# Another order of a hand-written list of stages, with some 70 stages on another engine, in an attention and two-MoE-block kernel on one core

## The chip, the cores and the metric

The kernel runs on one core of one Trainium2 chip. The metric is the device time of one execution in microseconds; 674.87 us is the median of three runs of the kernel before (674.87, 674.87 and 677.03).

The names of the engines in the rows: PE is TensorE (matrix products), PEld its weight loads, DVE is VectorE, ACT is ScalarE, POOL is GpSimd, and SP is SyncE, whose queue issues all transfers here.

## The reference, cut to what matters

Attention with four batches, eight heads, 512 local and 32 global rows of head size 64, and then two feed-forward blocks one after the other on all 2304 rows of width 512. A local row sees the local rows up to 32 places away and the 32 global ones; a global row sees all rows of its batch.

```python
s_g = scale * np.matmul(q_g, k_all.transpose(0, 1, 3, 2))
out_g = np.matmul(sm(s_g), v_all)
s_ll = np.where(np.abs(pos[:, None] - pos[None, :]) <= 32, s_ll, -1e9)
out_l = np.matmul(sm(np.concatenate([s_lg, s_ll], -1)), np.concatenate([v_g, v_l], axis=2))
...
h = x @ w_in                       # 512 -> 1024
solu = h * sm(h)
ln = (solu - mu) / np.sqrt(var + 1e-06) * g_ln
x = ln @ w_out                     # 1024 -> 512
...
h = x @ w2_in                      # 512 -> 2048
g = np.where(h >= 1, h, np.where(h <= -1, 0.0, (h + 1) ** 2 / 4))
out = g @ w2_out                   # 2048 -> 512
```

## The kernel before, in words

The 2304 rows are 17 tiles of 128: sixteen of local rows (four to a batch) and one with all global rows. A step is the work of one tile. For a tile's step the kernel does the attention, the first product of the first block (h, into two banks of PSUM), a softmax and a layer norm of it, transposes of the result, and, for two tiles at a time, the second product (y). The second feed-forward block follows after all tiles, from about 300 us on; it is not touched.

The float products run as three products of a high and a low part. A weight comes as a pair of words and has to be converted on the chip, piece by piece: 16 pieces of 128 x 1024 words, eight of the first weight (0 to 3 for the first half of h, 4 to 7 for the second) and eight of the second weight (8 to 15; 16 to 18 belong to the next block). The function `conv` (L166) has the steps of a piece: A strips the sign, C clamps, B shifts, D sets the sign and the exponent's top, F brings in bits of the lower word, m multiplies by the norm's gain (second weight only), H rounds to the high part, L subtracts it, which leaves the low part.

The tile framework orders most queues by itself, but up to the eighth step a list written out by hand, `SCRIPT` (L52), sets the order on every queue at once. It is read from the left, and `issue` (L945) issues each name's instructions, so each engine's queue has its own stages in the order of the list; across engines only data and buffers wait. (The list goes on into the ninth to fourteenth tile, since tiles ahead are prepared.) A name is a kind and a tile's number (a piece's number for A to L). A last letter v puts the stage on VectorE where it has a choice; without it the stage is on GpSimd (C, L, xl), or on ScalarE (A, H, Gc, Pa, Pb, xh, tha, thb). For Rn, Ie, ze, bn and nn it is the other way round: v puts them on ScalarE, without it they are on VectorE. The kinds that matter here:

- loads, on SyncE: q (scores' inputs of a tile, 0.85 MB), qg, v (values of a tile's windows, 1.05 MB, two buffers), vn (values of a batch), w (a piece, 0.52 MB), s and o for the next block's pieces. Three pieces in eight go to buffers of the pool, the others into rooms of the tensor xy, which later tiles and pieces use again (`ROOMS`, L80).
- attention: S scores (64 small products), M mask, R row maximum, Rn its scaling, Ea and Eb the exponentials of half the heads each, Ie and I the inverse of the sums, Ta and Tb transposes, Pa and Pb their copies, V the product with the values, X the norm, XT a transpose by blocks into xy. The same for the global rows: G scores, Gc their copy, gm, gn, ge, gi, gt, gp, gc, gv, go.
- first block: xh and xl the two parts of a tile of x; ha and hb the halves of h with the high part of x (eight products each), hA and hB with the low part (four each); mx maximum, ex exponential, ze and z inverse of the sum, u the product with h, bn, pw and nn the layer norm; ta and tb transposes, tha, thb, tla, tlb their high and low parts; ya, Ya, yb, Yb the quarters of y for two tiles, yca and ycb their copies.
- Z: three products of zeros on TensorE (`keep_warm`, L272).

Scores and h share two banks pairs of PSUM (the pool psH, `scores` L342, `hmm` L521): S and ha take them in turn, and wait until the last reader of the tile before the last is done, Eb for scores and u for h. G, T, V, gt, gv and the transposes take three other banks in turn (psA). The lines of the rows: L149 is every ScalarE activation but A, L140 most of VectorE's stages, L173 to L190 the steps of `conv`, L351 S, L404 and L406 G, L417 T, L432 V, L529 h, L270 y, L492 gv.

Of the kernel before, what the change touches and what calls it, by code (L numbers as in the profile page):

```python
# [1281 lines left out]
```

## Time and profile before

| what | us |
| --- | --- |
| median of three runs | 674.87 |
| lowest and highest | 674.87 and 677.03 |
| span of the profiled execution, first to last instruction | 673.8 |

| engine | busy us | share of the span | instructions |
| --- | --- | --- | --- |
| VectorE | 432.9 | 64% | 766 |
| ScalarE | 369.5 | 55% | 918 |
| GpSimd | 259.8 | 39% | 293 |
| TensorE weight loads | 577.5 | 86% | 6092 |

Matrix products are pipelined and their ends in the trace are modelled, so TensorE's busy time counts small gaps as work; its starts can be trusted, and its weight loads show how full it is. The list covers TensorE's first 160 us. In the page's 40 slices TensorE is busy 7, 6, 8 and 9 tenths in the first four and 9 or more from there on; VectorE is at 7 to 9 tenths in the first six slices, and the transfers move 321 to 358 GB/s in the first five.

### The profile page before, as it was taken

What the parts mean: (1) busy time and instruction counts of PE and PEld (TensorE: products, weight loads), DVE (VectorE), ACT (ScalarE), POOL (GpSimd) and SP (SyncE); (2) the same over time, 40 slices, a digit from 0 to 9 for tenths busy, and PEclk for the clock granted to TensorE, in tenths of its full rate; (3) what the DMA queues carried; (4) which work ended last, traced back from release to release, by engine and by line L of the source; (5) the groups of instructions that cost most, each with busy time, mean ns of one, the idle gap of its engine ahead of it and who ended that gap; (6) DMA issues with size and microseconds to landing.
All of it is one profiled execution on the core that took longest, in us unless ns stands there. A gap on an engine that the chain in (4) does not pass through costs nothing.

```text
span 673.8 us, 15103 instructions
## 1 busy us (share of the span) xinstructions
PE 655.2 (97%) x6089; PEld 577.5 (86%) x6092; DVE 432.9 (64%) x766; ACT 369.5 (55%) x918; POOL 259.8 (39%) x293
## 2 busy tenths in 40 slices
PE   7689999999999999999999999999999999999997
PEld 3467888989899889999999998998888888988986
DVE  5989987776787679654887679455655453333332
ACT  4888987556554244345666554554444466344443
POOL 2343463121112114203444676356776655222321
PEclk8979999999999999999999999999999999999999
DMA  8988854425752613301665341663333465744522
GB/s 321 358 348 333 343 203 159 165 65 164 288 193 92 254 32 125 95 1 32 187 188 186 128 125 63 217 220 126 125 126 125 134 210 190 237 136 157 170 81 80
DMA packets 29686, 114.24 MB, mean 170 GB/s; under 512 B 3376, under 2 KB 3888, under 8 KB 27056
## 3 DMA queue, kind: packets, MB, share of 16 engines
q1 hardware_dynamic: 29616, 113.28, 48.4%
q8 instruction: 48, 0.79, 0.5%
q14 instruction: 22, 0.18, 0.1%
HBM read 88.88 MB, written 24.38 MB: 168 GB/s over the span
## 4 chain that ended last, share of the span: by engine, by line
PE 90%; DMA 5%; DVE 3%; issue 1%; ACT 1%; SPq 0%; ACTq 0%
PE acc L270 26%; PE h L270 25%; PE yT L270 14%; PE h L529 13%; DMA vw<-in_vwin_dram 2%; PE plnT L594 2%; PE o L432 2%; DMA qkT<-in_qk_dram 2%; PE S L351 2%; PE pPT L417 2%; PE y L270 1%; PE og L492 1%; DVE xy L140 1%; PE G L404 0%; DVE w L180 0%
## 5 line engine op out<-in xcount | busy, mean ns | idle before, releaser
L270 PE MATMUL acc<-wo,g 128*128 128x512 f32 x816 | 211.3, 393 | 0.0
L270 PEld LDWEIGHTS acc<-wo,g 128*128 128x128 f32 x816 | 149.8, 188 | 23.2
L164 POOL TENSOR_TENSOR g<-xy,g 128x384 fp32r<-128x384 f32 (+1 forms) x65 | 62.8, 974 | 139.8 <-ACT g L149 122.4
L149 ACT ACTIVATE xy<-xy 128x384 f32<-128x384 f32 (+1 forms) x144 | 72.7, 505 | 71.5 <-DVE xy L140 68.5
L529 PE MATMUL h<-win,x 128*128 128x512 f32 x408 | 101.3, 400 | 0.0
L270 PE MATMUL yT<-lnT,wout 128*128 128x256 f32 x768 | 95.7, 284 | 0.0
L270 PEld LDWEIGHTS yT<-lnT,wout 128*128 128x128 f32 x768 | 93.4, 189 | 0.9
L529 PEld LDWEIGHTS h<-win,x 128*128 128x128 f32 x408 | 74.8, 188 | 15.9
L140 DVE TENSOR_TENSOR xy<-h,xy 128x384 f32<-128x384 f32 (+1 forms) x64 | 33.5, 524 | 62.1 <-PE h L270 60.9
L777 POOL TENSOR_TENSOR g<-xy,g 128x192 fp32r<-128x192 f32 x60 | 51.4, 876 | 54.2 <-ACT g L149 46.9
L149 ACT ACTIVATE g<-xy 128x384 fp32r<-128x384 f32 (+1 forms) x96 | 48.0, 500 | 18.7 <-DVE xy L140 16.7
L270 PE MATMUL h<-yT,w2i 128*128 128x384 f32 (+1 forms) x300 | 56.4, 334 | 0.0
L149 ACT ACTIVATE xy<-h 128x384 f32<-128x384 f32 (+1 forms) x64 | 30.0, 469 | 46.2 <-PE h L270 46.2
L270 PE MATMUL h<-yT,S 128*128 128x384 f32 (+1 forms) x288 | 54.9, 325 | 0.0
L270 PEld LDWEIGHTS h<-yT,w2i 128*128 128x128 f32 x300 | 52.5, 188 | 2.3
L140 DVE SCALAR_TENSOR_TENSOR xy<-h,xy 128x384 f32<-128x384 f32 (+1 forms) x48 | 26.1, 545 | 43.9 <-ACT xy L149 43.7
L270 PEld LDWEIGHTS h<-yT,S 128*128 128x128 f32 x288 | 48.8, 188 | 5.5 <-DVE xy L140 1.7
L149 ACT ACTIVATE e<-S,nm 128x128 f32<-128x128 f32 x128 | 45.3, 379 | 8.0 <-PE plnT L594 4.3
L571 POOL TENSOR_TENSOR rstd<-rstd,nhalf 128x1 f32<-128x1 f32 x17 | 11.4, 668 | 82.8 <-DVE rstd L140 49.6
L517 POOL TENSOR_TENSOR x<-xy,x 128x512 fp32r<-128x512 f32 x15 | 19.8, 1323 | 43.6 <-ACT x L149 35.5
L270 PE MATMUL h<-yT,lnT 128*128 128x384 f32 (+1 forms) x180 | 34.0, 334 | 0.1
L140 DVE SCALAR_TENSOR_TENSOR xy<-xy 128x384 f32<-128x384 f32 (+1 forms) x48 | 28.9, 602 | 7.8 <-ACT xy L149 7.8
(147 smaller groups left out, 1059.3 us busy)
## 6 DMA issues: line engine op xcount, KB each, us to landing
vw<-in_vwin_dram SPq DMA_DIRECT2D x16, 1024.0 KB, 7.0
wo<-w2d_o SPq DMA_DIRECT2D x32, 512.0 KB, 3.7
qkT<-in_qk_dram SPq DMA_DIRECT2D x15, 832.0 KB, 7.4
wraw<-in_w2i_dram SPq DMA_DIRECT2D x16, 512.0 KB, 3.7
wraw<-in_w2o_dram SPq DMA_DIRECT2D x16, 512.0 KB, 4.2
w2d_o<-wo SPq DMA_DIRECT2D x16, 512.0 KB, 5.1
w2d_s<-S SPq DMA_DIRECT2D x16, 512.0 KB, 5.5
S<-w2d_s SPq DMA_DIRECT2D x16, 512.0 KB, 5.9
```

The source lines that it names most:

```text
L140: self.last = getattr(nc.vector, name)(*args, **kw)
L149: vec.act = nc.scalar.activation(**kw)
L164: eng.tensor_tensor(out=lo, in0=src, in1=hi.bitcast(F32), op=ALU.subtract)
L270: mm(out=dst, lhsT=pairs[i][0][x], rhs=pairs[i][1][y], start=start and j == 0, stop=stop and j == 3 * n - 1, **kw)
L351: mm(out=S[32 * hp:32 * hp + 32, par, ci], lhsT=qT[r, hp, ci], rhs=kT[r, hp, w:w + 4].rearrange("p c d -> p (c d)"), start=True, stop=True)
L417: nc.tensor.transpose(ps[:, hp], eT[t][:, HP * par + hp], ident)
L432: mm(out=o[rows, ci, par], lhsT=PT[t][:, par, ci, rows], rhs=w[:, ci, D * h:D * h + D], start=True, stop=True)
L517: eng.tensor_tensor(out=xT[t][1], in0=x[:, :, n:n + P], in1=xT[t][0].bitcast(F32), op=ALU.subtract)
L529: mm(out=hps[t][:, half], lhsT=x[i][:, k], rhs=win[j][:, k, sl], start=not lo and j == 0 and k == 0, stop=lo and k == KD - 1)
L571: nc.gpsimd.tensor_tensor(sts[t].rstd, sts[t].rstd, nhalf, ALU.pow)
L594: nc.tensor.transpose(ps[:, k], ln[t][:, P * c:P * c + P], ident)
L777: eng.tensor_tensor(out=out, in0=x, in1=y, op=ALU.subtract)
```

## The change

The list holds the same 629 names, each once (and Z eight times), in another order on all queues, and 69 of them have their last letter added or taken away, so that these stages run on another engine of the two that they can use. The loads begin with pieces 0 and 5 and then the first tile's q; before, q of the first tile came first. Nothing else is changed: the same sums from the same values. The functions called are the same.

```diff
@@ -50,31 +50,32 @@
 SCRIPTED = 8
 
 SCRIPT = """
-Z0 q0 Z0 w0 qg0 S0 q1 w2 Z0 G0 w5 Gc0 S1 M0 A0v C0 R0 Rn0 B0 D0 F0 A2v Z0 G1 q2 M1 R1 C2 B2 D2 Ea0
-A5 v0 Rn1 Z0 C5 B5 H0 Ta0 Eb0 F2 Ea1 Z0 Pa0 S2 Gc1 G2 Gc2 M2 Eb1 D5 H2 F5 R2 q3 L0v L2v Z0 Z0 G3
-Gc3v Tb0 Ie0v w4 Rn2v I0 H5v Pb0 A4 C4 L5 V0 Ta1 Ea2 w1 S3 gm0 Pa1 A1v X0 Tb1 w7 Ie1v gn0 ge0 XT0 B4
-q4 qg1 Eb2 xh0 C1 A7v gt0 B1 M3 C7 q5 xl0 D4 B7 Pb1 gp0 D1 R3 F1 D7 F4 v1 G4 n0 S4 w6 H4v M4 w3 Rn3v
-Ie2v Ea3 Gc4 Ta2 Eb3 L4 V1 F7 H1 R4 I1 A6 Tb2 L1 H7 Pa2 S5 C6 Rn4v X1 v2 G5 Pb2 A3v L7 I2 XT1 q6 M5
-B6 Ea4 Ta3 C3 B3 Gc5 Eb4 R5 V2 v3 Tb3 S6 Rn5v D3 Ie4v X2 Pa3 Pb3 F3 w9 D6 H3v w11 G6 Gc6v Ea5 M6
-Ie3v Tb4 Eb5 F6 V3 I3 R6 w14 L3 XT2 A9v q7 H6 Ta4 X3 Pa4 L6 ha0 Rn6v v4 xh1 v5 A14 Ea6 C9 gi0 XT3 B9
-hb0 Pb4 D9 hA0 Eb6 hB0 C14v B14 F9 G7 Ta5 Gc7 Tb5 V4 mx0 v6 D14 w8 ex0 F14 m9 Ie6v S7 ze0 I6 z0 I4
-Pa5 u0 Pb5 M7 bn0v Ta6 xh2 pw0 X4 V5 Ie5v R7 Rn7v ha1 Ea7 gm1 Pa6 gn1 A11v XT4 Eb7 xl1 H9 Tb6 q8 I5
-m14 C11 hb1 hA1 vn0 gc0 L9 w10 nn0v hB1 xl2v B11 ha2 xh3 D11 mx1 ta0 F11 X5 hb2 ex1 ge1 A8v hA2 hB2
-H14v L14 ze1 tha0 z1 u1 tla0 Pb6 tb0 qg2 C8v m11 mx2 Ie7v V6 XT5 A10v bn1v thb0 gv0 pw1 S8 ex2 tlb0
-X6 v7 go0 ze2v z2 u2 nn1v Ta7 w13 gt1 B8 Pa7 C10 I7 xh4 xl3 D8 ta1 gp1 B10 H11 F8 ha3 m8 L11 tha1 M8
-v8 tb1 bn2v q9 Tb7 R8 thb1 H8 hb3 L8 hA3 Rn8v qg3 A13 D10 tlb1 w12 tla1 w15 Ea8 pw2 hB3 gc1 F10 XT6
-mx3 s0 ya0 nn2 m10 Pb7 G8 Eb8 ex3 C13 B13 V7 Gc8 D13 X7 H10 ze3v G9 F13 z3 Gc9 S9 A12v Ie8v Ta8 L10
-A15 u3 M9 bn3v R9 m13 xl4 C15 q10 Ya0 C12 tb2 B12 q11 ha4 s1 vn1 yca0 ta2 Pa8 hb4 Rn9 H13 thb2 hA4
-D12 F12 Ea9 B15 m12 tha2 D15 hB4 tla2 tlb2 Tb8 F15 G10 L13 Eb9 A16 H12v Gc10v mx4 S10 I8 L12 M10 s2
-Pb8 m15 G11 A17 XT7 v9 V8 pw3 Gc11 X8 v10 yb0 ex4 H15 ze4v C17 Ta9 L15v z4 Yb0 R10 Ie9v u4 xh5 nn3v
-bn4v C16v I9 ycb0 Pa9v ta3 XT8 xl5 pw4 gm2 ha5 Rn10 tha3 tb3 hb5 nn4 B17 gi1 hA5 hB5 tla3 B16 Ea10
-Eb10 thb3 Tb9 S11 xh6 Pb9 mx5 ex5 V9 ze5v tlb3 ta4 xh7 tha4v z5 u5 Ie10v A18 ya1 tb4 ha6 Ya1 v11 M11
-bn5v hb6 X9 xl6v D16 D17 R11 F16 F17 hA6 gn2 yca1 Rn11 C18v H16v Ea11 tla4 Ta10 hB6 yb1 Eb11 thb4
-tlb4 xh8v Tb10 q12 mx6 Pa10 B18 pw5 xl8 XT9 ge2 Pb10 I10 Ie11 D18 gv1 ex6 nn5v V10 ze6v X10 S12 Ta11
-q13 z6 Yb1 M12 F18 go1 Pa11 u6 tb5 R12 ycb1 thb5v ha7 tlb5 gt2 L16 hb7 ta5 gp2 tha5 bn6 gc2 Tb11 I11
-Rn12 xl7 pw6 H18v tla5 hB7 hA7 ya2 Ea12 nn6 Eb12 G12 Pb11v mx7 Gc12v S13 G13 ex7 gi2 Gc13v M13 Ie12v
-v12 V11 q14 o0 tb6 thb6 L18 ze7 Ya2 ta6 z7 R13 Rn13v Ea13 Eb13 s3 xd0 u7 xd1 tlb6 XT10 H17v tha6
-bn7v tla6 L17v Ie13 o1 X11 I12 I13 vn2 yca2 pw7 nn7 v13
+Z0 Z0 w0 w5 q0 A0 C0v B0 D0 qg0 A5 C5 B5 D5 F5 H5v S0 L5 F0 H0 L0 w2 q1 A2 Z0 G0 Gc0 G1 M0 R0 S1
+Rn0v Ea0 Eb0 C2v B2 D2 F2 H2v L2 w1 M1 R1 Ta0 Pa0 Rn1v Gc1v Ea1 q2 Eb1 A1v C1 B1 G2 Gc2 Ie1v q3
+S2 D1 M2 R2 F1 H1v G3 Gc3 w7 L1 A7v C7 gm0 gn0 S3 M3 R3 Rn3 Rn2v Ea2 Tb0 Pb0 Z0 ge0 gi0 Eb2 v0
+V0 w3 A3v C3 Ie0 w4 I0 X0 I1 Tb1 Ta1 XT0 Pa1 Pb1 B7 D7 F7 gt0 H7v Ea3 Eb3 B3 gp0 D3 F3 qg1 q4
+H3v L3 gc0 S4 M4 G4 Gc4 q5 S5 A4 L7 R4 Z0 M5 C4 v1 R5 G5 V1 X1 XT1 xh0 xl0 Gc5 n0 Tb2 Rn4 w14
+A14 C14 Ta2 Pa2v Ie3v B14 D14 F14 v2 Pb2 V2 Z0 Ie2v I2 X2 Ta3 Pa3v q6 m14 G6 Gc6v w6 Ea4 Eb4
+Rn5v Ea5 B4 D4 Ie4 A6v C6 Z0 XT2 Tb3 Pb3 Eb5 Tb4 F4 H4 L4 Ta4 B6 xh1 D6 F6 H6 Z0 S6 M6 R6 v3 V3
+I3 X3 Ie5v L6 ha0 hb0 XT3 Pa4 Pb4 w8 A8v C8 q7 xl1 G7 Gc7v gm1 v4 Rn6v H14 L14 Ea6 Eb6 Ie6v hA0
+hB0 mx0 ex0 V4 Ta5 vn0 S7 I4 X4 XT4 Tb5 Pa5 Pb5 ze0 z0 u0 bn0v gv0 go0 w9 gn1 ge1 A9v w10 M7 R7
+Tb6 Rn7 xh2v w11 A11v C9 pw0 ha1 hA1 hb1 hB1 C11v B11 D11 Ea7 Eb7 F11 w15 B8 D8 v5 V5 F8 nn0v
+qg2 Ta6 mx1 I5 ex1 Pa6 X5 XT5 Pb6 ze1 z1 u1 xh3 ha2 hb2 gi1 B9 m8 ta0 xl2 D9 F9 bn1v pw1 nn1v m9
+I6 v6 v8 tha0v tla0 V6 Ta7 X6 Pa7v q8 hB2 hA2 mx2 vn1 H9v H8 L8 tb0 L9 thb0 tlb0 tb1 thb1 ha3
+tlb1 ta1 tha1v m11 ex2 ze2v z2 tla1 A10 u2 gt1 gp1 Ie7v C10 B10 D10 F10 hb3 G8 xl3 Gc8v H11 v7
+xh4 m10 w12 A12 xl4 bn2v pw2 S8 gc1 hB3 hA3 M8 R8 q9 Rn8v H10v XT6 Tb7 mx3 G9 Gc9v Pb7 Ea8 nn2
+ya0 L10 L11v Ya0 ex3 ze3v z3 tb2 C12 u3 I7 ta2 xh5v Eb8 Ie8 xl5 bn3v pw3 S9 M9 R9 Rn9 tha2v tla2
+ha4 hA4 thb2 tlb2 yca0 w13 A13 Ea9 Eb9 q10 C13 B13 D13 s0 B12 hb4 D12 hB4 F12 m12 G10 Gc10v V7
+X7 xh6 A15 XT7 q11 ha5 Ta8 Pa8 Tb8 Pb8 F13 m13 mx4 ex4 ze4v H12v hA5 Ie9 nn3v I9 hb5 hB5 V8 H13
+C15 B15 D15 I8 X8 G11 L13v L12 yb0 F15 m15 Gc11 Ta9 H15 L15 Pa9 ta3 z4 u4 S10 bn4v Yb0 tha3 M10
+A16 pw4 R10 tla3 Rn10 tb3 thb3v XT8 ycb0 C16v gv1 Tb9 tlb3 mx5 go1 Ea10 Eb10 xh7v ya1 Ya1 v9
+Pb9v V9 s1 A17 gm2 gn2 s2 ex5 xl6 A18 C18 ze5 nn4 tb4 ta4 z5 u5 q12 B18 bn5v D18 F18 X9 XT9 S11
+C17 thb4 yca1 tlb4 qg3 B17 ha6 hb6 hB6 v10 pw5 Ta10 nn5v tha4v tla4 M11 R11 Rn11 Ea11 B16 v11
+hA6 mx6 Tb10 Pa10 Pb10 ex6 D17 F17 H17 Ie10 ge2 D16 Eb11 xd1 F16 ze6 z6 u6 bn6 pw6 yb1 Yb1 I10
+V10 X10 ycb1 Ta11 Pa11v ta5 tha5v tla5 q13 S12 gt2 ha7 M12 R12 tb5 gp2 gc2 gi2 hb7 XT10 thb5v
+tlb5 L17 G12 nn6 Gc12v xl7 H18 hA7 Rn12v Ea12 L18v Eb12 Ie12 Ie11v xh8 xl8 hB7 mx7 S13 M13 Tb11
+G13 xd0 Gc13v H16 ya2 L16 ex7 ze7v z7 u7 Pb11 bn7v pw7 o0 R13 tb6 ta6 q14 tha6v nn7 v12 Rn13v
+I11 o1 I12 tla6 V11 X11 thb6v tlb6 Ya2 s3 Ea13 Eb13 Ie13 I13 v13 vn2 yca2
 """
 
 ROOMS = [2, 3, 4, 0, 1, None, None, None, 2, 3, 4, 0, 1, None, None, None]
```

## Rows read from the trace of the kernel before

**Rows 1.** The page's busy time of each engine: us, share of the span, instructions.
```profile
PE 655.2 (97%) x6089; PEld 577.5 (86%) x6092; DVE 432.9 (64%) x766; ACT 369.5 (55%) x918; POOL 259.8 (39%) x293
```

**Rows 2.** Stretches: us, busy us by engine (PE, PEld, DVE, ACT, POOL), clock, DMA share, GB/s.
```profile
60.00:160.00 100.00, 99.88 (x1585) 87.98 (x1585) 82.48 (x156) 69.12 (x210) 36.65 (x35) 1.00 0.54 198
...
14.00:35.00 21.00, 14.36 (x415) 9.46 (x415) 19.76 (x37) 19.11 (x85) 6.58 (x8) 0.99 0.94 362
35.00:42.00 7.00, 5.93 (x142) 4.71 (x145) 5.08 (x10) 5.13 (x23) 3.32 (x4) 0.51 1.00 409
42.00:60.00 18.00, 16.24 (x437) 12.72 (x426) 17.77 (x37) 15.57 (x58) 5.14 (x6) 1.00 0.75 295
```

**Rows 3.** TensorE's timeline: start us, us, line, what, count, idle before and its releaser.
```profile
36.07 0.58 PE L432 MATMUL o<-vw,PT 128*32 128x64 f32 x10 [2.31 <-issue]
...
46.66 5.86 PE L529 MATMUL h<-win,x 128*128 128x512 f32 x24
...
54.96 1.10 PE L432 MATMUL o<-vw,PT 128*32 128x64 f32 x64 [0.83 <-DMA vw<-in_vwin_dram]
...
59.71 2.14 PE L529 MATMUL h<-win,x 128*128 128x512 f32 x8
...
135.08 0.65 PE L492 MATMUL og<-vn,PgT 128*32 128x64 f32 x32
...
136.74 1.10 PE L432 MATMUL o<-vw,PT 128*32 128x64 f32 x64
```

**Rows 4.** VectorE's timeline, the same columns (M0, F7, X1, M5, D6 to Gc6, F6, u0, gm1, D11).
```profile
6.31 0.70 DVE L140 TENSOR_TENSOR S<-S,masks 128x512 f32<-128x512 f32 x1 [5.20 <-PE S L351]
...
33.36 1.19 DVE L182 SCALAR_TENSOR_TENSOR w<-wraw,w 128x512 int32<-128x512 int32 x1
...
36.69 0.69 DVE L140 TENSOR_TENSOR xn<-o,rs 128x512 f32<-128x512 f32 x1 [0.90 <-PE o L432]
...
39.69 0.70 DVE L140 TENSOR_TENSOR S<-S,masks 128x512 f32<-128x512 f32 x1 [1.02 <-PE S L351]
...
43.90 0.68 DVE L180 SCALAR_TENSOR_TENSOR w<-wraw,w 128x512 int32<-128x512 int32 x1
44.50 0.41 DVE L186 CAST win<-w 128x512 fp32r<-128x512 f32 x1
44.84 0.48 DVE L140 COPY Sg<-G 128x128 f32<-128x128 f32 x2
...
46.03 0.81 DVE L182 SCALAR_TENSOR_TENSOR w<-wraw,w 128x512 int32<-128x512 int32 x1
...
56.00 1.28 DVE L140 SCALAR_TENSOR_TENSOR e<-e,s,h 128x1024 f32<-128x1024 f32 x1
...
59.54 1.28 DVE L140 TENSOR_REDUCE gnm<-Sg 128x2 f32<-128x1088 f32 x1
...
64.17 1.68 DVE L180 SCALAR_TENSOR_TENSOR w<-xy,w 128x512 int32<-128x512 int32 x1
```

**Rows 5.** Groups by form, 0 to 160 us: count, busy us, mean ns of one, idle before.
```profile
L140 DVE CAST lnT<-plnT 128x512 fp32r<-128x512 f32 x2 | 1.4, 684 | 1.3 <-PE plnT L594 1.3
...
L140 DVE COPY PT<-pPT 128x512 f32<-128x512 f32 x2 | 1.3, 660 | 0.0
L190 DVE TENSOR_TENSOR win<-w,win 128x512 fp32r<-128x512 f32 x2 | 1.3, 682 | 0.0
...
L190 POOL TENSOR_TENSOR win<-w,win 128x512 fp32r<-128x512 f32 x6 | 7.9, 1312 | 10.6 <-DVE win L186 8.7 <-ACT win L149 1.9
```

**Rows 6.** Timeline of SyncE's issues (q0, w9 with w11), and the stage that piece 5's landing released.
```profile
0.72 0.86 SPq L325 DMA_DIRECT2D qkT<-in_qk_dram  x2
...
12.93 0.68 ACT L174 ACTIVATE w<-wraw 128x512 f32<-128x512 f32 x1 [1.61 <-DMA wraw<-in_w1i_dram]
...
37.10 7.24 SPq L937 DMA_DIRECT2D xy<-in_w1o_dram  x2
```

## The prediction, made before the changed kernel was run

> **What bounds the kernel now.** I read the page first, for the shares, then the table of stretches, then TensorE's timeline for the place where it stops waiting, VectorE's timeline over the same stretch, the groups by form, and SyncE's issues last. By the page TensorE is busy 97% of the span and VectorE 64% [rows 1]. The stretches part this: from 60 to 160 us TensorE is busy 99.88 of 100 us, but from 42 to 60 us only 16.2 of 18, and its weight loads 12.7, which tell better how full it is [rows 2]. So what the list can win lies ahead of 60 us, and is worth what it makes the dense stretch begin earlier, corrected for work that changes sides of that point. The reader is to see in TensorE's timeline three things: the first h product (ha0) at 46.66; V4 at 54.96, held by a window of values; and ha1 at 59.71, after which nothing waits [rows 3]. VectorE tells why. It is busy 17.8 of the 18 us from 42 to 60 [rows 2], and u0, the last reader of the bank that ha1 is to write, starts only at 56.00 [rows 4].
>
> I count in places of VectorE's queue: a stage takes its length less about 0.08 us by which neighbours overlap (D6 at 43.90 is 0.68 long and the next starts at 44.50; the cast there takes 0.34, the pair of copies at 44.84 0.40) [rows 4]. By that count 42.0 us of stages stand ahead of u0 in the old list, so VectorE had lost 14.0 us by then, 6.3 of it ahead of its first stage [rows 4].
>
> **Part 1, the engines.** Of 69 stages with another engine, VectorE takes seven copies to lnT (0.60, from 0.68) and a net three of PT (0.58), three pairs of Sg (0.40) and two of xT (0.34), about 6.8 with some small sums, and gives away three sign strips (0.34), a net one low part of a weight and two of x (0.60), 2.8. With the smaller spacings of single stages I take +5.0 us; ScalarE loses 5.8, GpSimd gains a low part of a weight and two of x, 3 x 1.25 = 3.7 [rows 4, 5]. From 60 to 160 us VectorE is idle 17.5 of 100 us, GpSimd 63 [rows 2]: that covers both there. Ahead of 60 us nothing covers VectorE.
>
> **Part 2, what stands ahead of u0.** New ahead of it: C0, C2, H1, H2, H7, A6, A8 (7 x 0.34), Gc1 and Gc7 (0.8), Pa2 and Pa3 (1.1), X4 and XT4 (1.2), gm1 (1.2), gc0 and small ones (0.6): 7.3. No longer: A0, A2, A9, C14, H4, B9 (6 x 0.34), D9, F9, L0, L2 (4 x 0.60), Gc3 and small ones: 5.1. Net **+2.2 us** [rows 4]. The same count ahead of F6 gives +3.1 (14's three stages, 1.5, moved ahead, M6 behind).
>
> **Part 3, the pieces lead.** SyncE issues w0 and w5 ahead of q0, which had been first at 0.72 [rows 6]. q0 lands some 3 us later, since 1.05 MB (two tiles of 128 x 1024 words) go ahead of it; S0, G0 and the first exponentials start later by as much. On TensorE that costs nothing by itself: it waits anyway. Its cover is VectorE, which had its first stage at 6.31 (M0) [rows 4] and now starts with C0, near 5.1 by my estimate: less than q0's 0.85 MB must land, then ScalarE's sign strip runs. Eight stages of pieces 0 and 5 fill the wait. (The list's eight keep-warm steps stay eight, two of them at its head; they cost TensorE only time in which it waits.) M0 then stands at about 10.0 with 3.8 us done: 6.2 lost, against 6.3 at M0 and 8.4 some stages on. q1 keeps its place (3.41 MB, landed by 12.93 [rows 6]), so M1 comes near 15, with about 7 lost, some 1.5 less than before.
>
> **Part 4, waits that go and come.** In the old list V1 was held 2.31 us in its middle for nothing the profile shows; VectorE paid 0.90 and 1.02 for it at X1 and M5 [rows 3, 4]. The hold may fall elsewhere. New: B1 stands behind C1, on GpSimd behind L2 (0.65); G2 is now ahead of S2, and takes banks that Gc1 on VectorE frees (up to 0.7 at M2); Gc7 waits for G7 (0.9). Together VectorE's saving up to u0 lies between **0** (the new waits take all) and **5.4** (no hold and no collision); I take **2.0**: 1.5 from the start, 1.9 from the hold, 0.96 from M2's old wait, less 2.3 for the new ones. u0 starts at 56.0 + 2.2 - 2.0 = 56.2, ends at 57.5, and ha1 starts at **57.7**. TensorE's own side agrees: F6 starts at 46.0 + 3.1 - 1.6 = 47.5, piece 6 ends 2.6 us later (F6, cast, GpSimd's 1.31 [rows 5]), hb0, which needs it at its seventh matmul, starts near 48.7, and 9.0 us of products stand between hb0 and ha1. Those now hold gv0 (1.66) in place of V5 (1.10), so ha1 2.0 earlier with 0.6 us more done is a lead of **2.6 us** [rows 3].
>
> **Part 5, the transfers.** SyncE is in order: in the old list w11 waited for F3's buffer from 37.10 to 44.0 with q7 and v4 queued behind it, and V4 waited for v4 [rows 3, 6]. Now F3 comes 7.6 us of VectorE's work sooner, w9 to w15 stand behind v4, and 17.6 MB go up to v4. From 3.41 MB at 12.93, at the 409 GB/s of 35 to 42 us or the 362 of 14 to 35 [rows 2, 6], v4 lands at 47.5 to 52.0; V4 wants it at 53. q2 and q3 wait for S0 and S1, with 0.5 to 0.9 MB queued ahead of them: no cost, or up to 1 us, within the bounds. vn0, wanted at 55.5, lands at 50.3 to 55.
>
> **Part 6, after ha1.** S8 takes the bank that u2 frees, no longer u1's. VectorE ends u2 near 79.4 and S8 is due at 79.1: 0.3 us lost. Ya0 needs L11, now on VectorE near 87.8, and S9 needs u3 near 89: both within 0.5 us of their need, on either side. Sum: 2.6 - 0.3 = **2.3 us**. All behind the eighth step is unchanged, and TensorE stays full there [rows 2]. The profiled execution lasts 673.8 us in its span and 1.1 us lie around it, which gives the median of 674.87. So 673.8 - 2.3 + 1.1 = **672.6**.
>
> **A rule against it.** F7 started at 33.36, inside a GpSimd subtraction, and took 1.19 us in place of 0.68; D11 at 64.17 took 1.68 [rows 4]; GpSimd's subtraction is 1.31 long [rows 5]. The Trainium skill, "SBUF — State Buffer", who interferes with whom, says that a VectorE operation with two SBUF inputs and a GpSimd operation that reads SBUF exclude each other, whoever starts first. The trace agrees. By that rule GpSimd's ten such operations ahead of hb0 (seven before) would raise 2.1 us of collisions to 3.0, and the sum would be 673.5.
>
> **The rivals.** *The lead is kept whole*: VectorE saves 4.5 or more of the 5.4, and ha1 is bound by TensorE's products at 56.0. For it: the hold has no cause in the list. Against: collisions stay. Lead 4.3: **670.5**. *VectorE is held by GpSimd, slower*: the new list puts 2.9 us more of GpSimd's work ahead of L6, just where D and F stand. Held stages cost VectorE 2.1 us ahead of u0 and 2.5 from there to u3 before (stages over their kind's median; F7 and D11 are the type [rows 4]). At twice that u0 starts 2.1 later and u3 4.6: S9 then waits and the lead is gone (676); at 2.5 times it is **678.5**. It decides from 1.8 times on. Against: in the old list only two to six of such stages met. (The page on SBUF above is this mechanism's.) *The clock*: from 35 to 42 us it was granted at 0.51, the level of 1.2 GHz, ahead of ha0 [rows 2]. If such a stretch of 7 us falls on h0 and V4, half of it is lost: 672.6 + 3.5 = **676.0**. Against: TensorE's early work is about as thin, not thinner. *It does not do what it says*: new waits take all, u0 at 58.2, lead 0.6, about 674.5; it is the end of the forecast's own bounds.
>
> **How the numbers follow.** A measurement here tells about 0.5% (3.4 us) from no change. Forecast with its bounds (670.8 to 674.5): 0.43, of which 0.10 below 671.5. Lead kept whole: 0.30, all of it faster. Clock: 0.10, within. Held by GpSimd: 0.17, slower. Faster 0.30 + 0.10 = 0.40; same 0.33 + 0.10 = 0.43; slower 0.17. The range takes in the forecast, the clock and most of the whole lead, with a small part of the last: 668.8 to 677.0.
>
> **What would show it.** Right: VectorE's first stage near 5, M1 near 15, u0 near 56.2, ha1 near 57.7 with V5 behind h1, no hold of SyncE near 37 to 44, and TensorE full from ha1 on. Wrong: u0 after 58 or ha1 bound by something else (an exponential, vn0); D and F longer than 1 us in numbers; TensorE waiting at S8, S9 or Ya0; the granted clock low after 45.

## The result: one per cent slower

The changed kernel takes 682.74 us (median of four runs, 682.0 to 684.12), the kernel before 675.95 in the same session: a ratio of 1.0101, 95% interval 1.0081 to 1.0121. The spans of the profiled executions are 679.9 and 673.8 us. The forecast, 672.6 with a range to 677.0, was wrong in its sign. The mean granted clock is 0.992 in both traces, so the clock does not make the difference between them.

The profile after, first the page's busy times (to be held against [rows 1]) and the stretches ([rows 2]). All line numbers are higher by one; in the kernels of the experiments they are lower by one than before.

```profile
PE 659.5 (97%) x6092; PEld 577.4 (85%) x6092; DVE 441.1 (65%) x784; ACT 364.1 (54%) x897; POOL 261.2 (38%) x296
...
14.00:35.00 21.00, 13.80 (x414) 9.82 (x414) 19.41 (x39) 17.53 (x79) 5.37 (x6) 0.84 1.01 399
35.00:42.00 7.00, 4.21 (x153) 3.15 (x152) 6.82 (x12) 4.23 (x21) 3.98 (x5) 1.00 0.96 367
42.00:60.00 18.00, 18.00 (x372) 12.66 (x362) 15.89 (x32) 12.61 (x51) 7.34 (x7) 0.91 1.02 401
60.00:160.00 100.00, 98.52 (x1549) 83.24 (x1539) 88.80 (x169) 68.11 (x202) 34.40 (x36) 1.00 0.44 160
```

The reader is to see three things. From 42 to 60 us TensorE is busy in every us and yet does no more than before (weight loads 12.66, before 12.72). From 60 to 160 us its loads fall from 87.98 to 83.24: it is less full there. And the transfers, which paused before (295 GB/s from 42 to 60), now run at 401 GB/s until 60 us.

TensorE's timeline after (start, length, line, what, count; in brackets the idle time before and its releaser), to be held against [rows 3]:

```profile
40.29 0.86 PE L433 MATMUL o<-vw,PT 128*32 128x64 f32 x42 [1.31 <-DVE PT L141]
41.65 0.54 PE L433 MATMUL o<-vw,PT 128*32 128x64 f32 x22 [0.50 <-issue]
42.12 1.31 PE L277 MATMUL Z<-zero 128*128 128x512 bf16 x3
43.23 1.06 PE L418 MATMUL pPT<-ident,e 128*128 128x128 f32 x4
44.22 0.68 PE L405 MATMUL G<-qkT,qkg 64*32 64x128 f32 x16
44.83 1.25 PE L277 MATMUL Z<-zero 128*128 128x512 bf16 x3
45.91 1.47 PE L418 MATMUL pPT<-ident,e 128*128 128x128 f32 x12
47.22 0.81 PE L277 MATMUL Z<-zero 128*128 128x512 bf16 x3
47.96 1.16 PE L352 MATMUL S<-qkT 64*32 64x128 f32 x64
49.04 1.10 PE L433 MATMUL o<-vw,PT 128*32 128x64 f32 x64
...
56.43 1.10 PE L433 MATMUL o<-vw,PT 128*32 128x64 f32 x64
...
59.72 0.42 PE L493 MATMUL og<-vn,PgT 128*32 128x64 f32 x14
61.41 0.49 PE L493 MATMUL og<-vn,PgT 128*32 128x64 f32 x18 [1.27 <-issue]
...
63.32 3.04 PE L530 MATMUL h<-win,x 128*128 128x512 f32 x12
```

Of the kernel before, V2 and S6:

```profile
40.99 1.50 PE L432 MATMUL o<-vw,PT 128*32 128x64 f32 x64
...
43.00 1.16 PE L351 MATMUL S<-qkT 64*32 64x128 f32 x64
```

V2 is at 40.29 and starts 0.7 us earlier than before. Between it and ha0 (50.08, behind V3 at 49.04) stand three keep-warm steps (Z) and waits. Then gv0 stops for 1.27 us in its middle for nothing that the profile shows, and ha1 comes at 63.32, before at 59.71.

To say where the time goes I take a stage's start on TensorE less all the dense work ahead of it (each kind at the interval that it has where nothing waits: h 1.87, S 1.09, V 1.03, a group of transposes 0.36; the zeros count as no work). That is how late TensorE is, in us:

| at | V2 | ha0 | ha1 | ha2 | Ya2 (end of the list) | span |
| --- | --- | --- | --- | --- | --- | --- |
| before | 26.12 | 27.15 | 29.96 | 30.15 | 32.30 | 673.8 |
| after | 25.78 | 30.57 | 32.94 | 33.17 | 37.94 | 679.9 |
| growth against before, from the column to its left | | +3.8 | -0.4 | 0.0 | +2.6 | +0.5 |

So the loss has two places in these two traces: 3.8 us between V2 and ha0, and 2.6 us in the dense stretch behind ha2. The two figures are not equally sure. Three kernels further down (seams moved, loads later, gv0 later) have the changed kernel's lists up to ha0, apart from loads issued after 43 us in one of them, and with the changed kernel's own trace that makes four traces of nearly the same work: ha0 comes at 49.55 to 51.09, that is 2.9 to 4.4 us later than before, and V2 to ha0 takes 8.9 to 10.4 us. From ha2 to Ya2 all twelve kernels in the new order with the new engines lie 2.0 to 3.1 us above the trace before.

VectorE's timeline after, against [rows 4] (C0 and M0; D7, F7, H7, then B3, D3, F3; Pa3; F6; u0 and what follows it):

```profile
5.23 0.43 DVE L177 TENSOR_SCALAR w<-w 128x512 f32<-128x512 f32 x1 [4.12 <-ACT w L175]
...
10.24 0.69 DVE L141 TENSOR_TENSOR S<-S,masks 128x512 f32<-128x512 f32 x1
...
29.87 0.69 DVE L181 SCALAR_TENSOR_TENSOR w<-wraw,w 128x512 int32<-128x512 int32 x1
30.60 0.69 DVE L183 SCALAR_TENSOR_TENSOR w<-wraw,w 128x512 int32<-128x512 int32 x1
31.32 0.43 DVE L187 CAST win<-w 128x512 fp32r<-128x512 f32 x1
31.66 0.42 DVE L179 TENSOR_SCALAR w<-w 128x512 int32<-128x512 int32 x1
32.12 0.69 DVE L181 SCALAR_TENSOR_TENSOR w<-xy,w 128x512 int32<-128x512 int32 x1
32.84 0.69 DVE L183 SCALAR_TENSOR_TENSOR w<-xy,w 128x512 int32<-128x512 int32 x1
...
44.33 0.69 DVE L141 COPY PT<-pPT 128x512 f32<-128x512 f32 x1 [1.40 <-PE pPT L418]
...
49.31 1.67 DVE L183 SCALAR_TENSOR_TENSOR w<-wraw,w 128x512 int32<-128x512 int32 x1
...
59.77 1.28 DVE L141 SCALAR_TENSOR_TENSOR e<-e,s,h 128x1024 f32<-128x1024 f32 x1
...
63.05 0.29 DVE L141 TENSOR_TENSOR ogn<-og,gs 128x128 f32<-128x128 f32 x1 [1.99 <-PE og L497]
```

D7 and F7 are 0.69 long and follow each other at 0.73, and F7 reads what D7 wrote; before, D6 at 43.90 was followed at 44.50 by a stage that did not read it, 0.60 later [rows 4]. I call such a pair dependent neighbours. Ahead of u0 the old order has 11 of them, the new one 42: the new list runs a piece's steps one behind the other.

### The profile page after: what moved, and what is told of

The parts are those of the page before. It is cut to its first block, busy times and chain, and to the rows that moved or that the text cites. A ratio compares the mean times of both kernels' runs of the same rounds, so it can differ in the third digit from the quotient of the medians.

```text
span 679.9 us, 15117 instructions
## 1 busy us (share of the span) xinstructions
PE 659.5 (97%) x6092; PEld 577.4 (85%) x6092; DVE 441.1 (65%) x784; ACT 364.1 (54%) x897; POOL 261.2 (38%) x296
## 4 chain that ended last, share of the span: by engine, by line
PE 87%; DVE 9%; issue 2%; ACT 1%; DMA 1%; POOL 1%; SPq 0%; DVEq 0%; ACTq 0%; POOLq 0%
PE acc L271 25%; PE h L271 24%; PE yT L271 14%; PE h L530 13%; PE plnT L595 2%; PE o L433 2%; PE pPT L418 2%; PE S L352 2%; DVE S L141 1%; DVE nm L141 1%; DVE w L181 1%; DVE w L183 1%; DVE xy L141 1%; PE y L271 1%; PE og L493 1%
## 5 line engine op out<-in xcount | busy, mean ns | idle before, releaser
L518 POOL TENSOR_TENSOR x<-xy,x 128x512 fp32r<-128x512 f32 x17 | 21.9, 1286 | 46.5 <-ACT x L150 37.1
L271 PEld LDWEIGHTS h<-yT,lnT 128*128 128x128 f32 x180 | 31.6, 188 | 2.0 <-DVE xy L141 0.5
```

The lines of the kernel that those rows point to most:

```text
L271: mm(out=dst, lhsT=pairs[i][0][x], rhs=pairs[i][1][y], start=start and j == 0, stop=stop and j == 3 * n - 1, **kw)
L518: eng.tensor_tensor(out=xT[t][1], in0=x[:, :, n:n + P], in1=xT[t][0].bitcast(F32), op=ALU.subtract)
```

## The experiments

### Parts of the change alone

Loads alone: the old list with SyncE's new order; and the reverse, the new list with SyncE's old order.

```diff
-SyncE: q0 w0 qg0 q1 w2 w5 q2 v0 q3 w4 w1 w7 q4 ... q6 v3 w9 w11 w14 q7 v4
+SyncE: w0 w5 q0 qg0 w2 q1 w1 q2 q3 w7 v0 w3 w4 ... q6 w6 v3 w8 q7 v4 vn0 w9 w10 w11 w15
```

> The old list with one queue altered: SyncE issues its loads in the changed list's order (pieces 0 and 5 lead, w9 to w15 behind v4). Nothing else is moved, so VectorE still begins with M0. Theory 1: the loads cost nothing by themselves in the changed kernel; here M0 waits for the later q0 (some 3 us) with nothing to fill the wait, so up to 3 us slower, and less where the wait for v4 falls away; the hold of SyncE from 37 to 44 us goes. Rival (the loads alone are the loss): 5 us slower or more.

> The changed list with SyncE's loads in the old list's order: q0 first, the pieces behind it, w9 and w11 ahead of v4. All other queues keep the changed order, so VectorE's first stages, C0 to F5, wait for pieces that now come later. Theory 1 (the order of the loads belongs to the order of the stages): slower than the changed kernel by 3 us or more, since VectorE begins at 7.5 or later and M0 stands behind eight stages of weights. Theory 2 (the early pieces delay the scores and cost more than they give): faster than the changed kernel by 1 us or more.

Measured: 693.86 (1.0269, 1.0242 to 1.0296), and 711.04 (1.0525, 1.0498 to 1.0551). In the first M0 starts at 10.01 us in place of 6.31 with nothing ahead of it. My guess of up to 3 us was far too small. Where the rest of its 18.5 us arises was not followed. The clock is a rival for part of it: the mean granted clock is 0.975 in the first trace and 0.961 in the second.

Engines alone (the old order with the 69 switches; the diff shows this one) and order alone (the new order, its loads included, without them):

```diff
-... M0 A0v C0 R0 Rn0 B0 D0 F0 A2v Z0 G1 q2 M1 R1 C2 ...
+... M0 A0 C0v R0 Rn0v B0 D0 F0 A2 Z0 G1 q2 M1 R1 C2v ...
```

> The old order on all queues, with the 69 stages on the engines that the changed list gives them. Dependent neighbours on VectorE stay few (8 ahead of u0). Theory 1 (dependent neighbours, and TensorE's neighbours after ha1, both made by the order): between 1 us faster and 2 us slower than the old kernel, since VectorE has about 5 us more to do, of which 2 to 3 lie ahead of u0. Theory 2 (the switched stages cost it, through GpSimd's holds): at least 4 us slower, near 680.

> The changed order on all queues, with every stage on the engine that the old list gave it: none of the 69 switches. Theory 1 (the switches and the order add up: the old order with the switches is 9.4 us slower than the old kernel, the changed kernel 6.8): the order alone is 2 to 3 us faster than the old kernel, near 673. Theory 2 (the order needs its switches, the engines are chosen for it): slower than the changed kernel, 684 or more. Theory 3 (the order is the loss, by dependent neighbours on VectorE, of which it has 43 ahead of u0, and by TensorE's neighbours): 679 to 684.

Measured: 684.82 (1.0129, 1.0109 to 1.0149) and 703.67 (1.042, 1.0396 to 1.0443). The parts do not add up: 18.5 us for the loads, 9.4 for the engines, 28.6 for the order with its loads, and 6.8 for all together. Each list is one whole, and a part of the new one costs more in the old one than all of it. So the loss cannot be handed to one of the parts.

### Neighbours on VectorE

Chaining: only VectorE's order in the old list is altered, so that dependent neighbours ahead of u0 rise from 11 to 34. Spreading: the same in the new list, 42 to 10; and in the old list, 11 to 3.

```diff
 old list, chained
-VectorE: L0v L2v Gc3v I0 H5v gm0 A1v X0 gn0 XT0 B4 A7v B1 M3 D4 B7 D1 R3 F1 D7 F4
+VectorE: L0v L2v Gc3v I0 gm0 gn0 A1v X0 XT0 B4 D4 A7v B1 D1 F1 M3 R3 B7 D7 F7 F4
 new list, spread
-VectorE: XT0 B7 D7 F7 H7v B3 D3 F3 H3v gc0 M4 R4 M5 R5
+VectorE: XT0 D7 B3 F7 M4 H7v D3 gc0 F3 H3v R4 M5 Rn4 R5
```

> The old list with one queue altered: VectorE's order up to u3 is rearranged so that stages that read the result of the stage directly ahead rise from 11 to 34 ahead of u0 (18 to 52 ahead of u3). No stage is added, no engine changed, all other queues keep their order. Theory 1 (dependent neighbours, 0.13 us each): u0 some 2.5 to 3 us later than 56.0, and the time 2 to 3 us above the old kernel's. Theory 2 (GpSimd's holds or new waits): no stage count changes, so u0 within 0.7 us of 56.0 and the time within 1 us.

> The changed list with one queue altered: VectorE's own order, in which a stage that reads the result of the stage directly ahead of it now mostly has another stage put between the two. Such pairs fall from 42 to 10 ahead of u0 and from 89 to 14 in the whole list; all other queues keep the changed kernel's order. Theory 1 (a stage behind the one that makes its input starts about 0.13 us later): u0 near 55.8 instead of 59.77, ha1 near 59.7, and the time about 3 us below the changed kernel, near 679, not wholly back to 675 since the products after ha1 keep their slower neighbours. Theory 2 (GpSimd holds VectorE's stages, or the new waits do): u0 within 0.7 of 59.8 and the time within 1 us of 682.7. Theory 3 (the loss is all in TensorE's order): the lead at ha1 appears, but the time stays within 1 us of 682.7.

> The old list with one queue altered: 16 stages of VectorE moved so that stages that read the result of the stage directly ahead fall from 24 to 5 in the whole list, 11 to 3 ahead of u0. Theory 1 (in the old order VectorE sets the pace up to u0, as chaining its stages showed: 23 more such pairs cost 3.5 us): 8 pairs at 0.13 are 1 us, so 0.5 to 1.2 us faster than the old kernel. Theory 2 (spread stages come late for others, as in the changed list, where spreading brought nothing): within 0.5 us or slower.

Measured: chained 679.56 (1.0052, 1.0035 to 1.0069), some 3.5 us slower, a little over what was expected; in its trace u0 is 1.4 us later (57.40, expected 2.5 to 3), ha1 0.6 (60.27), and ya0 3.0 (87.92, before 84.95), so most of it reaches TensorE behind ha1. The new list spread: 683.52 (1.0109, 1.0091 to 1.0126), nothing gained, with u0 at 60.41 where 55.8 was expected. The old list spread: 674.84 (1.0001, 0.9987 to 1.0014), nothing either. So chaining costs, but taking it away pays nothing. TensorE's timeline of the new list spread shows where it went:

```profile
59.77 0.42 PE L491 MATMUL og<-vn,PgT 128*32 128x64 f32 x14
62.62 0.49 PE L491 MATMUL og<-vn,PgT 128*32 128x64 f32 x18 [2.42 <-issue]
```

The stop in gv0 is 2.42 us in place of 1.27, and ha1 is 1.2 us later than in the changed kernel (64.53). The same in the old list spread: S6 comes 2.0 us earlier (40.97, before 43.00), and V3 stops behind its fourth product:

```profile
43.96 0.30 PE L431 MATMUL o<-vw,PT 128*32 128x64 f32 x4 [0.73 <-DVE Sg L139]
45.90 1.09 PE L431 MATMUL o<-vw,PT 128*32 128x64 f32 x60 [1.63 <-issue]
```

### What the stops are

The page lists a queue of its own for instructions ("q8 instruction: 48, 0.79, 0.5%"): 48 packets of 16 KB for TensorE's 12184 instructions, so 254 instructions, or 127 products with their weight loads, in a packet. I set each packet's time in the trace beside the stops. Some of them (products counted from TensorE's first):

```
kernel                 product  stops at  for   packet         goes on  after the packet
before                   601     33.76   2.31   33.64-34.59    36.07    1.47
loads alone              604     37.22   2.88   37.82-38.83    40.10    1.27
engines alone            604     37.18   0.72   35.38-36.44    37.90    1.46
zeros at the head        602     34.76   2.86   35.10-36.12    37.62    1.50
changed                  604     35.51   0.97   34.05-35.14    36.48    1.34
changed                 1112     60.15   1.27   58.98-60.05    61.41    1.36
new list spread         1112     60.20   2.42   60.19-61.29    62.62    1.33
old list spread          858     44.27   1.63   43.63-44.61    45.90    1.29
```

The stops come at the same counts in the old list and the new (near 350, 604, 731, 858, 1112, 1366, all a multiple of 127 apart, whatever stage stands there: V1 in the old order, G5 or S5 in the new one; a count can be short by a few records that are missing). Leaving out those where the profile names another releaser, there are 47 stops of over 0.4 us in the 20 profiled kernels; 46 of them, in 19 kernels, are at these counts and end 1.2 to 1.6 us after such a packet. (The other is in the order-alone kernel, at product 185.) So I read the 2.31 us in V1 of [rows 3], for which the prediction found no cause, and the 1.27 us in gv0 as one thing: TensorE has run through its instructions and waits for the next ones. The Trainium skill, "Runtime: NRT & Kernel Launch", section "Instruction fetch mechanics", says that an engine's instructions are refilled in blocks of 16 KiB over a DMA queue of the sequencer's own, and that crossing a block is mostly hidden. The traces agree on the size, and by count on the hiding: 46 of the 960 packets in the 20 traces leave such a stop. But all 46 lie in the first 80 us, and the longest takes 2.88 us.

### Keep-warm steps and TensorE's neighbours

The last four Z to the head of the list; that together with VectorE's spreading; and the last three Z left out:

```diff
-... V2 Z0 Ie2v I2 X2 Ta3 ... A6v C6 Z0 XT2 Tb3 ... F6 H6 Z0 S6 ...
+... V2 Ie2v I2 X2 Ta3 ... A6v C6 XT2 Tb3 ... F6 H6 S6 ...
```

> The changed list with its last four keep-warm steps (Z, three products of zeros each) taken from their places behind S5, V2, G6 and Ta4, at 34 to 48 us, to the head of the list, where TensorE has nothing to do. Nothing else moves, and TensorE keeps as many instructions. Theory 1 (these steps stand on the path: TensorE does 0.8 to 1.3 us of zeros while Ta3, Tb3 and S6 could run, and VectorE waits for Ta3's copy): ha0 1.5 to 2.5 us earlier than 50.08, and the time 1.5 to 2.5 us below the changed kernel. Theory 2 (the steps stand in time in which TensorE waits anyway, as my prediction had it): ha0 and the time within 0.7 us of the changed kernel's. Theory 3 (they keep the clock up): slower than the changed kernel by up to 2 us, with more time at the low clock.

> The changed list with both edits: VectorE's dependent neighbours spread, and the last four keep-warm steps at the head. Theory 1 (on this path VectorE and TensorE take turns, and what spreading saves was lost at TensorE's keep-warm steps and at products that come late): ha0 near 47.5 and the time 3 us or more below the changed kernel. Theory 2 (spreading costs as much in new waits as it saves): no better than the edit of the keep-warm steps alone, within 0.7 us of it or slower.

> The changed list without its last three keep-warm steps (nine products of zeros that nobody reads, behind V2, G6 and Ta4 at 42 to 48 us); nothing else moves, and the products ahead of V2 keep their places in TensorE's stream. Theory 1 (they stand on the path to ha0): ha0 1.5 to 2.5 us earlier than 50.08 and the time 1.5 us or more below the changed kernel. Moving them to the head gave no gain because it also moved the point, 604 products into TensorE's stream, at which it stood still for 2.86 us in place of 0.97. Theory 2 (they are needed for the clock): ha0 less than 0.7 us earlier, more time at the low clock between 42 and 60 us, and no gain or a loss.

Measured: 684.92 (1.0137, 1.0115 to 1.0158), 684.67 (1.0138, 1.0114 to 1.0162), and 682.77 (1.0114, 1.0100 to 1.0127): no gain, and ha0 is at 51.05, 49.03 and 49.70, where the first theories had 47.6 to 48.6, 47.5 and again 47.6 to 48.6. With the three left out V2 to ha0 takes 7.9 us in place of 9.8, but a new stop stands in V3, and that in gv0 is longer:

```profile
47.65 0.35 PE L431 MATMUL o<-vw,PT 128*32 128x64 f32 x9
48.78 0.98 PE L431 MATMUL o<-vw,PT 128*32 128x64 f32 x55 [0.78 <-issue]
...
62.36 0.33 PE L491 MATMUL og<-vn,PgT 128*32 128x64 f32 x9 [2.35 <-issue]
```

How much the three zeros cost is not shown. In the four traces with the changed kernel's lists up to ha0, V2 to ha0 takes 9.8, 8.9, 9.1 and 10.4 us; in the three that differ from these by the missing zeros (this one, the same with the seams moved, the same with gv0 later) it takes 7.9, 9.0 and 10.1. The two ranges overlap, and ha0 lies at 49.55 to 51.09 in the one and 49.40 to 50.38 in the other.

The dense stretch: on TensorE a group that follows another kind can start later. In the changed kernel a transpose ahead of global scores takes 0.53 (88.43 to 88.96), before one ahead of h takes 0.35 (94.07 to 94.42):

```profile
88.43 0.60 PE L418 MATMUL pPT<-ident,e 128*128 128x128 f32 x4
88.96 0.45 PE L405 MATMUL G<-qkT,qkg 64*32 64x128 f32 x16
```
```profile
94.07 0.60 PE L594 MATMUL plnT<-ident,e 128*128 128x128 f32 x4
94.42 2.11 PE L529 MATMUL h<-win,x 128*128 128x512 f32 x8
```

Counted pair by pair, such seams make 1.4 of the 2.6 us. The test moved 13 TensorE stages behind ha1, alone and with the three Z left out:

```diff
-TensorE: ... hb1 hB1 V5 Ta6 ha2 hb2 ta0 V6 Ta7 hB2 hA2 ... tb2 ta2 S9 ha4 hA4 hb4 hB4 G10 ...
+TensorE: ... hb1 V5 Ta6 hB1 ha2 hb2 V6 Ta7 hB2 ta0 hA2 ... S9 tb2 ha4 hA4 ta2 hb4 G10 ...
```

> The changed list with one queue altered: TensorE's own order behind ha1, where 13 of its stages change places with near neighbours so that fewer dear seams are left (a group of products that follows another kind of group can start 0.1 to 0.2 us later: transposes ahead of scores or values 0.53 each in place of 0.36, scores next to the global scores 0.2 cheaper). Counted by the intervals of the traces so far, the seams from ha1 to the end of the list fall from 4.7 us to 3.2. Theory 1 (after ha1 the changed kernel loses 2.5 us more than the old one, and 1.4 of it are these seams): 1 to 1.5 us below the changed kernel. Theory 2 (the loss behind ha1 is made by waits that busy time hides, and moving stages makes new ones): within 0.5 us of it or slower.

> Both edits: the changed list without its last three keep-warm steps, and with the TensorE order of fewer seams behind ha1. Theory 1 (both are losses of TensorE's own queue and add up): 2.5 to 4 us below the changed kernel, near 679, that is half of the loss. Theory 2: no better than the better one of the two.

Measured: 686.22 (1.0157, 1.0139 to 1.0174) and 682.60 (1.0119, 1.0094 to 1.0144). The lateness from ha2 to Ya2 grows by 4.87 and 4.82 us in them, in the changed kernel by 4.77: the transposes that I moved became 0.17 cheaper each, and others, with a wait ahead of tb0, dearer by as much. So the seams are real at their places, but that they make the 2.6 us is not shown. Nor is it one wait: stage by stage, no interval from ha2 to Ya2 is more than 0.4 us over the shortest of its kind, in either kernel, and the 2.6 us are the sum of many small lengthenings. The kernels in the new order with the new engines show 4.2 to 5.2 there, the old list 2.15 (with VectorE spread 2.60). Most of the loss of the first of these kernels lies ahead of the stretch that was to be tested: up to ha1 its lists are the changed kernel's own, and yet ha1 is at 66.74 in place of 63.32. Its TensorE timeline at gv0:

```profile
60.75 0.42 PE L491 MATMUL og<-vn,PgT 128*32 128x64 f32 x14
63.50 0.80 PE L491 MATMUL og<-vn,PgT 128*32 128x64 f32 x18 [2.32 <-issue]
64.22 0.44 PE L495 MATMUL og<-vg,PgT 32*32 32x64 f32 x8
64.59 1.08 PE L491 MATMUL og<-vn,PgT 128*32 128x64 f32 x32
```

The stop at product 1112 took 2.32 us in place of 1.27, and from 63.3 to 70.1 us the granted clock was at the lower level, 1.2 GHz, so that the second half of gv0 took 1.08 in place of 0.65. So one trace's figure for ha1 can differ by 3 us from another's with nothing changed ahead of it.

### The stop in front of ha1

```diff
 loads later
-SyncE: ... v4 vn0 w9 w10 w11 w15 v5 qg2 v6 v8
+SyncE: ... v4 vn0 w9 w11 v5 v6 w10 w15 qg2 v8
```

> The changed list with SyncE's order altered between vn0 and v8: w9, w11, v5, v6, w10, w15, qg2 in place of w9, w10, w11, w15, v5, qg2, v6. v6 waits for V4's buffer until about 57.5, so w10 and w15 (1.05 MB) come behind that point and the queued transfers end near 58.8 in place of 61.3 us. Theory 1 (TensorE's instruction packet for product 1112 waits behind queued data): the packet starts near 58.0 in place of 58.98, the stop inside gv0 shrinks from 1.27 us to 0.5 or less, ha1 0.5 to 1 us earlier, and the time 0.5 to 1 us below the changed kernel. Theory 2 (the packet is late because TensorE runs through some 200 short products at this place, whatever the transfers do): the stop stays over 1 us, the time within 0.7 us.

> The changed list with three edits: VectorE's dependent neighbours spread, the last three keep-warm steps left out (nine products of zeros that nobody reads), and the loads w10 and w15 behind v6. Theory 1 (the first two save 2 us or more ahead of gv0, and the stop at product 1112 swallowed it): ha1 near 61, 2 us earlier than in the changed kernel, and the time 2 us or more below it. Theory 2 (the stop comes however the loads are queued): ha1 at 63 or later, no gain.

Measured: 680.85 (1.0084, 1.0065 to 1.0103) and 680.86 (1.0082, 1.0061 to 1.0104). With the loads later gv0 runs through, and ha1 is 1.8 us earlier. The packet for product 1112 starts at 57.08, when TensorE is at its 1028th product; in the changed kernel it starts at 58.98, at the 1094th.

```profile
59.19 0.90 PE L491 MATMUL og<-vn,PgT 128*32 128x64 f32 x32
60.02 0.31 PE L495 MATMUL og<-vg,PgT 32*32 32x64 f32 x8
60.27 0.65 PE L491 MATMUL og<-vn,PgT 128*32 128x64 f32 x32
60.85 0.31 PE L495 MATMUL og<-vg,PgT 32*32 32x64 f32 x8
61.10 0.66 PE L416 MATMUL pPT<-ident,e 128*128 128x128 f32 x4
61.51 1.87 PE L528 MATMUL h<-win,x 128*128 128x512 f32 x7
```

From 42 to 60 us the transfers ran at 360 GB/s in place of 401, and the span is 2.2 us shorter. In the measured times the gain is 1 to 2 us against the changed kernel, which two intervals of this width do not part; but the three kernels with the loads later, one of them further down, lie at 680.7 to 680.9, and the nine others in the new order with its engines and its early loads at 682.6 to 686.2. So the later loads do save; that they save by the missing stop is not shown, for one of the three stops all the same (below). The other way to take the stop away, gv0 behind Ta6 and go0 behind I5, alone and with the three Z left out:

> The changed list with gv0 on TensorE moved from ahead of ha1 to behind Ta6, ahead of ha2, and go0, which reads it, moved on VectorE from behind u0 to behind I5. Eighty short products leave the stretch ahead of ha1, and product 1112 then falls into the long products of h. Theory 1 (the stop inside gv0 is what ha1 waits for): no stop over 0.6 us ahead of ha1, ha1 at 61.0 to 61.5 in place of 63.32 (u0 sets it), VectorE goes on 2 us earlier behind u0, and the time 1.3 to 2 us below the changed kernel. Theory 2 (what is saved here comes back at the next short products): stops move to V6 or gv0's new place, within 0.7 us.

> As the kernel before it (gv0 behind Ta6, go0 behind I5), and the last three keep-warm steps left out as well. Theory 1: the 1.4 to 1.9 us that those steps cost between V2 and ha0 are no longer swallowed at product 1112: ha1 near 60.5, and the time 2.5 to 3.5 us below the changed kernel, about half of the loss. Theory 2: no better than either edit alone.

Measured: 684.21 (1.0131, 1.0105 to 1.0156) and 684.81 (1.0147, 1.0126 to 1.0169). The stop is gone and ha1 is earlier (62.55 and 61.33), and in the first gv0 at its new place (72.78) waits 2.76 us, by the profile for a copy on ScalarE: theory 2, though by a wait, not by a stop.

Two of the switches, in the loads-later kernel undone and in the old list done alone:

```diff
-Pa2v ... Pa3v          (new list: on VectorE)
+Pa2 ... Pa3            (on ScalarE, Pa3 behind Rn5)
```

> The kernel in the changed order with w10 and w15 behind v6, and in it two of the 69 switches undone: Pa2 and Pa3 on ScalarE again (Pa2 ahead of Pb2, Pa3 ahead of Ea5), so that VectorE has 1.2 us less to do ahead of u0 and V2 and V3 no longer wait for VectorE's queue. Theory 1 (these two switches are a good part of what is lost between V2 and ha0): ha0 1 us or more earlier than 49.55, u0 1 us earlier than 59.15, and the time 0.7 to 1.5 us below the 680.85 of that kernel. Theory 2 (that stretch is bound by TensorE's own stops and clock): ha0 within 0.5 us and the time within 0.7 us of it.

> The old kernel with two of the 69 switches alone: Pa2 and Pa3 on VectorE, in their old places of the list. Theory 1 (two copies of 0.55 in VectorE's full queue ahead of u0, and V2 and V3 behind them): u0 1 to 1.5 us later than 56.00 and the time 0.7 to 2 us above the old kernel's. Theory 2 (what they cost VectorE falls into its waits): within 0.5 us.

Measured: 680.74 (1.0075, 1.0058 to 1.0091) and 676.62 (1.0013, 0.9997 to 1.0029). Undone, ha0 is 0.9 us earlier (48.68) and u0 0.8 (58.31), as theory 1 said; the time is the same. TensorE again stops at its 1112th product, for 1.76 us, and ha1 is where the changed kernel has it (63.27), though the time is 2 us less:

```profile
60.51 0.44 PE L491 MATMUL og<-vn,PgT 128*32 128x64 f32 x17 [1.76 <-issue]
```

Done alone, u0 is 2.2 us later (58.21) and the time 1.1 us longer, which the interval can't tell from nothing.

All kernels in the new order with the new engines and loads that keep gv0 ahead of ha1, side by side, with the granted clock from 60 to 71 us:

| kernel | ha0 | gv0 | stop at product 1112 | clock | ha1 |
| --- | --- | --- | --- | --- | --- |
| changed | 50.08 | 59.72 | 1.27 | 1.00 | 63.32 |
| seams moved | 50.98 | 60.75 | 2.32 | 0.69 | 66.74 |
| VectorE spread | 50.12 | 59.77 | 2.42 | 1.00 | 64.53 |
| zeros at the head | 51.05 | 61.38 | 2.00 | 0.84 | 66.63 |
| the same, VectorE spread | 49.03 | 58.87 | 2.35 | 0.69 | 64.88 |
| three Z left out | 49.70 | 59.47 | 2.35 | 1.00 | 64.10 |
| the same, seams moved | 49.40 | 59.04 | 2.55 | 0.69 | 65.05 |
| loads later, Pa2 and Pa3 back | 48.68 | 58.33 | 1.76 | 0.84 | 63.27 |
| loads later | 49.55 | 59.19 | none | 1.00 | 61.51 |
| loads later, spread, three Z left out | 49.76 | 59.40 | none | 1.00 | 61.58 |

Every kernel with the early loads stops there, for 1.3 to 2.6 us, whether gv0 comes at 58.9 or at 61.4; so the stop is not simply what an early gv0 has to give back. In five of the eight that stop, the clock falls to the lower level within 0.9 us of the stop's end, and from ha1 to ha2 they take 7.8 to 8.8 us; all five others take 7.2. So ha1 is set in part by how long the stop lasts and by what the clock does behind it, and these differ from trace to trace.

## Why the prediction was wrong, point by point

**What held.** The start: first stage at 5.23 (forecast 5.1), M0 at 10.24 (10.0), M1 at 15.26 (15). The count ahead of u0: 44.3 us of stages against 42.0, so +2.3 (forecast +2.2). The transfers: v4 landed at 51.09 (47.5 to 52.0), vn0 at 53.71 (50.3 to 55), and SyncE's hold from 37 to 44 us was gone (its waits near there end at 38.0 and 42.2). ScalarE lost 5.4 us (5.8), GpSimd gained 1.4 (3.7), and VectorE 8.2 (5.0). (The stages that Part 1 lists as taken over come to 7.8 us, not 6.8; its +5.0 is 7.8 less 2.8.)

**The step that failed first** is the saving of Part 4, "I take 2.0". VectorE's lag at u0 (start less the stages ahead) went from 13.99 to 15.52: a loss of 1.5, so the term was mis-sized by 3.5, and u0 came at 59.77, not 56.2 (59.2 to 61.2 in the four traces that share these lists, of which one has other loads after 43 us). Its parts: the start saved 1.1 (forecast 1.5) and the waits 1.0 (3.68 to 2.67), stages longer than their kind 0.3, single spacings 0.3; but dependent neighbours cost 5.42 in place of 1.20, 4.2 more. Part 2 counted every stage at its length less 0.08, read from D6 with an independent stage behind it, and that is the error in it: D7, F7 and H7 in a row stand 0.13 wider. The bounds of that term, 0 to 5.4, had no room below zero. That this bookkeeping is not the whole path is shown by the spread kernel: it has 10 such pairs, and waits of 5.47 in place of 2.67 and three stages more ahead of u0 took back all that it saved and more (60.41).

**"They cost TensorE only time in which it waits"**, said of the keep-warm steps, was wrong at 42.12 at least: Ta3 stands behind those zeros, and VectorE waits 1.40 us for it (44.33). Two of the three steps there lie in a spell of the low clock (1.2 GHz, 42.3 to 45.7 us, lengths 1.31 and 1.25 in place of 0.81). What the three cost in sum is not shown, since leaving them out gave no gain that stands out of the traces' spread. I had looked only at how many there are, not at what stands beside them.

**Part 5** asked when transfers land and not what else needs the transfers' engines. With 401 GB/s up to 60 us TensorE's own instruction packet for product 1112 started at 58.98, and gv0, which my sum moved ahead of ha1 as 0.6 us of more work, took 3.2 in place of 1.66. With 1.05 MB moved to later in that queue the packet started 1.9 us sooner (57.08), the stop was gone in two kernels of three, and the times fell by 1 to 2 us.

**Part 6, "TensorE stays full there"**, failed by 2.6 us from ha2 on. Busy time (98.52 of 100) could not show it, and I read [rows 2] as if the stretch were a property of the kernel and not of the order in it. Its cause is partly open: it is made of many small lengthenings; seams are seen, their sum is not shown.

**The rivals.** The slower rival, VectorE held by GpSimd, gave a time that was nearer (678.5), but its mechanism was not it: stages held beyond their kind cost 1.58 us ahead of u0, before 1.90. The longest is F6, 1.67 us, started inside GpSimd's subtraction at 49.14 to 50.43, as the Trainium skill, "SBUF — State Buffer", who interferes with whom, has it. The clock was low at 18.4 to 25.2 and at 42.3 to 45.7 us and not again ahead of 160, and its mean is that of the kernel before; but in several of the experiments it fell behind the stop in gv0, which the rival had not placed there. I gave 0.17 to slower because each rival was one mechanism; what came was several small ones, each outside the sum.

**What stays open.** Up to ha0 the changed kernel loses some 3 us, and between V2 and ha0 every kernel in the new order loses 2.3 us or more, against 1.0 in the trace before, but 1.7 to 4.0 in the other kernels of the old order. Dependent neighbours, the two copies on VectorE, the zeros and the stops at products 604, 731 and 858 all stand at that place. A share for each is not shown: taking away one of them moved ha0 by little more than the traces of one list differ.

## What to carry to other kernels

In a list written by hand, price a stage by its neighbour too: one that reads the result directly ahead of it on VectorE cost 0.13 us more, 42 of them 5.4 us. A program of many short products can run out of instructions: look for stops "for nothing" at equal counts of an engine's instructions, and try to keep big transfers out of the queue where they fall. Here several limits lay within a us or two of each other, and a delay passed on while most savings did not; such an edit of the order deserves more weight on slower than 0.17. And before a gain of 1 to 2 us is read from one trace, compare two traces of the same work: here they differed by 1.5 us at ha0 and by 3.4 at ha1.
